# Two blocks of K and V fewer in the third pass: p k vᵀ summed on GpSimd and TensorE in the second

## The chip, the cores and the metric

The kernel runs on one core of a Trainium2 chip. The metric is the device time of one execution in microseconds (us). The core has five engines, each with its own instruction queue: TensorE (PE; its weight loads are shown as PEld), VectorE (DVE), ScalarE (ACT), GpSimd (POOL) and SyncE (SP), and 16 DMA engines between device memory and the on-chip memory SBUF. TensorE writes to PSUM, a small accumulator memory of eight banks.

## What is computed

One decode step (one token, model width 1024) through two rounds of attention and feed-forward, forward and backward:

```python
x = x + A(layernorm(x))      # layer 1: attention, 32 query heads, 4 K/V groups, 65536 keys, head width 128
x = x + B(layernorm(x))      # layer 2: squared-ReLU feed-forward, 1024 -> 3584 -> 1024
x = x + A(layernorm(x))      # layer 3: the same weights and the same caches
x = x + B(layernorm(x))      # layer 4
# outputs: x, and the gradients to the input, k_cache, v_cache, wq, wo, w1, b1, w2, b2

def A(x):
    q = (x @ wq), as 32 heads of 128; k, v = k_cache, v_cache, each group serving 8 heads
    p = softmax(q k^T / sqrt(128)); o = p v
    return o @ wo
```

For a head with the output gradient dO, the gradient to the query is dq = sum over keys c of p_c (dO·v_c − δ) k_c, with δ = dO·o. As dO is the same for all keys, any set of keys S gives

sum over S of p_c (dO·v_c − δ) k_c = (sum over S of p_c k_c v_cᵀ) dO − δ (sum over S of p_c k_c).

The two sums on the right need p, k and v, and neither dO nor δ.

## The kernel before

The caches hold 4 groups x 65536 keys x 128 in bf16, 67 MB each. They do not fit on the chip and are streamed four times:

- **pass 1** (layer 1 forward) and **pass 2** (layer 3 forward), `attn_fwd`: K and V;
- **pass 3** (layer 3 backward, the part that leads to dq of layer 3), `attn_bwd3`: V and K;
- **pass 4** (the rest of layer 1's backward, and the gradients to K and V of both layers), `attn_bwd4`: V and K, and 134 MB are written.

Between the passes lie dense stretches (`dense12`, `dense23`, `dense34`), in which the feed-forward layers run on streamed weights.

**Tiling.** 128 keys are a chunk, 512 chunks are a group. 8 chunks are an item, the step of a pass's loop: a pass has 256 items. 32 chunks (J) are a block of 1 MB, the unit of DMA; two neighbouring blocks that are loaded together are a pair of 2 MB. 64 chunks (HB) make a score tile, 128 chunks (SU) a softmax unit, with a running maximum from unit to unit.

**The arena.** All blocks lie in one SBUF tensor `arena` of 20 granules of 1 MB (`NSLOT` = 12 plus 8). The 8 granules are the planes that keep exp(scores) of each layer and group (`E(lay, g, ...)`), each held from its group's start on until pass 4 has used it. In pass 2 the planes of layer 1 are held throughout and those of layer 3 one after the other, so that K and V have 12 granules and up to three not yet held planes. `kv8` (L351) loads a block or a pair at its first use in program order into the granules that have been free longest (`take_pair`, `take_one`); `kv_done` (L377) gives a block's granule back after its last item, unless the block is in `KV["keep"]`. At the end of pass 2, 7 blocks of V are kept for pass 3. The loads (L361 one block, L366 a pair, L459 weights) are issued from SP's queue in program order; each waits there for its granule's last reader, so that the distance between the release of a granule and its next use is how far a load can run ahead.

**Pass 2.** In `pipeline` (L847) step i runs `kT` of item i (8 transposes of K on PE, L1031, copied from PSUM to a `kt` tile by DVE or ACT, L164 and L161), `kS` of item i−2 (8 score matmuls, L1049), and `v8` of item i−36 (8 matmuls of V with E, L1132), and then `bg.step`: one piece of background work (the q projections of the coming groups, the output projections of the finished ones), if there is any. A unit's statistics (maximum, exponentials) run some steps later: small DVE instructions, two small PE instructions (L1086, L1096) whose PSUM tiles come from `ps_mv` (one buffer, tag `mv`), and the exponentials on ACT (L1114). The order of the instructions on PE, DVE and ACT is the program's order (`manual_schedule`); GpSimd has no work in passes 1 to 3.

**Pass 3.** Step i runs `vT` of item i (8 transposes of V, L1225), `vS` of item i−2 (8 matmuls with dO, L1251), and `k8` of item i−13 (8 matmuls of K with ds = p (dO·v − δ), L1279), which sum dq of one unit in PSUM; `fold` adds the unit to the group's sum with the unit's softmax factor (`fold_dq`).

**Dense23** transposes chunks of the weight w1 into 8 `wt` buffers of its own (`ch_turn`, L1715).

Of the kernel before, what the change touches and what calls it, by code (L numbers as in the profile page):

```python
# [16 lines left out]
P = 128  # L17
# [3 lines left out]
def kernel(  # L21
# [57 lines left out]
    slotp = ctx.enter_context(tc.tile_pool(name="slotp", bufs=1))  # L79


    PS = {}

    def open_psum(stack, name, pass4=False):
        PS["pool"] = stack.enter_context(tc.tile_pool(name=name, bufs=1, space=PSUM))
# [12 lines left out]
        return PS["pool"].tile(shape, F32, name="ps_acc", tag="acc", bufs=1)  # L98

    def ps_mv(shape, dtype=F32):  # L100
        if PS["pass4"]:
            return ps_tr(shape, dtype)
        return PS["pool"].tile(shape, dtype, name="ps_mv", tag="mv", bufs=1)

    def ps_bg(shape):
        return PS["pool"].tile(shape, F32, name="ps_bg", tag="bg", bufs=1)
# [244 lines left out]
    def kv8(t, g, c8):  # L351
        hb, j = divmod(c8, J)
        key = (t, g, hb)
        have = KV["have"]
        if key not in have:
            i = None
            if NOW["pairs"] and hb % 2 == 0 and (t, g, hb + 1) not in have and key not in KV["halves"]:
                i = take_pair()
            if i is None:
                sl = Slot("blk_" + t, load=True)  # L360
                nc.sync.dma_start(out=sl.t.rearrange("p (j d) -> p j d", d=DH), in_=half(KVIN[t], g, hb))  # L361
                have[key] = sl
            else:
                for h in range(2):
                    have[(t, g, hb + h)] = Slot("blk_" + t, at=i + h)
                nc.sync.dma_start(out=wide(i).rearrange("p (j d) -> p j d", d=DH), in_=KVIN[t][g][hb // 2])  # L366
        return have[key].t.rearrange("p (j d) -> p j d", d=DH)[:, j:j + 8, :]
# [9 lines left out]
    def kv_done(t, g, c8):  # L377

        key = (t, g, c8 // J)
        if c8 % J == J - 8 and key not in KV["keep"]:  # L380
            KV["have"].pop(key).free()

    def order_by_unit(desc, unit):
        out = []
        gs = range(G)
        us = range(C // unit)
        for g in (reversed(gs) if desc else gs):
            for u in (reversed(us) if desc else us):
                out += [(g, c8) for c8 in range(u * unit, (u + 1) * unit, 8)]
        return out  # L390
# [18 lines left out]
    DV_LAG = TLEAD + 1  # L409
    V_LEAD = 4 * J // 8  # L410
    ITEMS = [order_by_unit(False, SU), order_by_unit(True, SU), order_by_unit(False, HB), order_by_unit(True, J)]
    V_SHIFT = lambda k: min(V_LEAD, max(0, (k - V_LEAD) // 3))
    TOUCH = [touch_order(ITEMS[0], [("k", 0), ("v", FWD_LAG)]), touch_order(ITEMS[1], [("k", 0), ("v", FWD_LAG)]),
             touch_order(ITEMS[2], [("v", 0), ("k", B3_LAG)]), touch_order(ITEMS[3], [("v", V_SHIFT), ("k", B4_LAG + V_LEAD)])]
# [6 lines left out]
    def start_pass(p):  # L421
        KV["keep"] = plan_keep(p)
        KV["turned"] = KV.get("next", set())
        KV["next"] = set()
        KV["turn"] = {0: "k", 2: "v"}.get(p)
        NOW["pairs"] = p < 3
        KV["halves"] = set(TOUCH[p][-8:] + (TOUCH[p][:18] if p else []))

    def f_cols(ap, nb):
        return ap[:, bass.ds(512 * (nb // 4) + nb % 4, P, step=4)]  # L430
# [353 lines left out]
    class Background:  # L784
# [8 lines left out]
        def step(self, i):  # L793
            while self.later and i >= self.later[0][0]:
                self.add(*self.later.popleft()[1:])
            while self.urgent:
                r = next(self.urgent[0][1], "end")
                if r == "end":
                    self.urgent.popleft()
                    continue  # L800
                if r == "wait":
                    break
                return
            while self.normal and self.done < self.total * i / self.steps:
                if next(self.normal[0], "end") == "end":
                    self.normal.popleft()
                else:
                    self.done += 1
                    return

        def add(self, gen, key=None):
            self.urgent.append((key, gen))
# [27 lines left out]
    def first_at(n, fn):  # L840
        TASKS.setdefault(NOW["i"] + n - 0.5, []).append(fn)
# [2 lines left out]
        for fn in TASKS.pop(i, ()):  # L844
            fn()

    def pipeline(items, stages, bg, end=(), holds=(), lead=None):  # L847

        def due(lag):
            at = {}  # L850
            for k, it in enumerate(items):
                at.setdefault(k + lag + LEAD if lead is None or lag >= 0 else k + ~lag + lead(k), []).append(it)
            return at
        LEAD = 0 if lead is None else lead(len(items))
        when = [due(l) for _, l in stages]
        maxlag = max(l for _, l in stages) + LEAD
        for i in range(len(items) + maxlag):
            NOW["i"] = i
            NOW["wide"] = NOW["pairs"]
            for at, k in holds:  # L860
                if i == at:
                    hold(k)
            tasks(i - 0.5)
            for n, (fn, lag) in enumerate(stages):
                for it in when[n].get(i, ()):
                    fn(*it)
                if n == 0:
                    tasks(i)
            bg.step(max(0, i - LEAD))
            NOW["wide"] = False  # L870
            NOW["step"] += 1
            for before, fn in end:
                if i == len(items) + maxlag - before:
                    fn()
        while TASKS:
            k = min(TASKS)
            NOW["i"] = int(k + 0.5)
            tasks(k)
# [128 lines left out]
    def attn_fwd(p, L, on_group, bg, end=()):  # L1007
# [113 lines left out]
        def v8(g, c8):  # L1121
            su = c8 // SU
            vb8 = kv8("v", g, c8)
            if c8 % SU == 0:
                state["ps_o"] = ps_acc([P, 8, R])
            if c8 % SU == SU // 2:
                unit_sums(g, su)
            ps_o = state["ps_o"]
            for i in range(8):
                c = c8 + i  # L1130
                w = min(8, (su + 1) * SU - c)
                NOW["ps_o"] = nc.tensor.matmul(ps_o[:, 0:w, :], lhsT=vb8[:, i, :], rhs=E(p, g, c, w),  # L1132
                                               start=(c % SU == 0), stop=(c % SU == SU - 1), skip_group_check=True)
            kv_done("v", g, c8)
            if (c8 + 8) % SU == 0:
                first_at(1, lambda: unit_end(g, su, ps_o))

        def unit_sums(g, su):

# [43 lines left out]
        holds = [(k * n + 2, plane(p, g)) for k, g in enumerate(order) if k > 0]  # L1183
        if p == 0:
            holds.append((len(items) - 40, plane(1, ITEMS[1][0][0])))
        with tc.manual_schedule(engines=ORDERED):
            pipeline(items, [(kT, 0), (kS, TLEAD), (v8, FWD_LAG)], bg, end, holds)
        st.close()


# [16 lines left out]
    def attn_bwd3(p, L, on_group, bg, end=()):  # L1207
# [5 lines left out]
        state = {}  # L1213
        gfirst = {g: next(c8 for gg, c8 in items if gg == g) for g in range(G)}
        glast = {g: [c8 for gg, c8 in items if gg == g][-1] for g in range(G)}

        def vT(g, c8):
            bg.need(g)
# [50 lines left out]
        def k8(g, c8):  # L1269
            kb8 = kv8("k", g, c8)  # L1270
            dsT = state[("ds", g, c8 // HB)]
            if c8 % SU == 0:
                state["ps_dq"] = ps_acc([P, 8, R])
            ps_dq = state["ps_dq"]
            for i in range(8):
                c = c8 + i
                s = c % HB
                w = min(8, HB - s)
                nc.tensor.matmul(ps_dq[:, 0:w, :].rearrange("p a b -> p (a b)"), lhsT=kb8[:, i, :],  # L1279
                                 rhs=dsT[:, s:s + w, :].rearrange("p a b -> p (a b)"),  # L1280
                                 start=(c % SU == 0), stop=(c % SU == SU - 1), skip_group_check=True)
            kv_done("k", g, c8)
            if (c8 + 8) % SU == 0:
                su = c8 // SU

                def fold():
                    fold_dq(L, g, su, ps_dq[:, 0, :], gfirst[g] // SU == su, glast[g] // SU == su, dspool)
                    if glast[g] // SU == su:
                        on_group(g)
                first_at(1, fold)  # L1290
# [294 lines left out]

    def open_dense(name):
        st = ExitStack()
        DENSE["pool"] = st.enter_context(tc.tile_pool(name=name, bufs=1))
        return st

# [89 lines left out]
    def on2(g):  # L1680
        if g != lastg[1]:
            bg.add(g_wo(L3, x3, g))
    attn_fwd(1, L3, on2, bg, [(3, pre_load("wo3", lambda: wo_slabs(lastg[1], 2)))])
    bg.drain()

# [29 lines left out]
    def ch_turn(s, js=range(4), to=None):  # L1715

        n = ch_pe(s)
        for j in js:
            pt = ps_tr()
            for kc in range(n):  # L1720
                nc.tensor.transpose(pt[:, kc, :], ch_cols(s, kc, j), ident_b[:, :])
            wt = DENSE["pool"].tile([P, 8, P], BF, name="wt", tag="wt", bufs=8)
            (nc.vector.tensor_copy if (to[j] if to else j == 3) else nc.scalar.copy)(out=wt[:, 0:n, :], in_=pt[:, 0:n, :])
            w1t[(s, j)] = wt

# [132 lines left out]
            bg.add(g_dn(L3, dn3, g, g == firstg[2]))  # L1858
    attn_bwd3(2, L3, on3, bg, [(10, pre_load("wq3", lambda: wq_slabs(lastg[2], 2)))])
    bg.drain()  # L1860


    reset_load()
# [202 lines left out]
```

## Time and profile before

| | |
|---|---|
| median of 3 runs | 1934.61 us (1930.21 to 1937.13) |
| profiled execution: its time; span in the trace | 1938.19 us; 1936.3 us |
| pass 2, first score matmul (L1049) to last V matmul (L1132) | 424.8 to 740.7 us |
| pass 3, first to last matmul with dO (L1251) | 780.0 to 1107.5 us |
| busy share of the span: PE, PEld, DVE, ACT, POOL | 82%, 67%, 61%, 54%, 7% |
| read from device memory, written | 617.62 MB, 165.69 MB |
| mean DMA rate over the span | 407 GB/s |

The page gives one execution: the busy share of each engine, the span in slices, the DMA queues, the chain of work that ended last, and the costliest groups of instructions with what they waited for. A matmul's shown duration is modelled and overlaps with its neighbours'; the spacing of starts tells more than the duration. A window's row gives, for each engine, the busy us and, in brackets, the number of instructions; then the granted clock of TensorE (1.00 is full speed), the DMA share and the rate.

### The profile page before, as it was taken

What the parts mean: (1) busy time and instruction counts of PE and PEld (TensorE: products, weight loads), DVE (VectorE), ACT (ScalarE), POOL (GpSimd) and SP (SyncE); (2) the same over time, 40 slices, a digit from 0 to 9 for tenths busy, and PEclk for the clock granted to TensorE, in tenths of its full rate; (3) what the DMA queues carried; (4) which work ended last, traced back from release to release, by engine and by line L of the source; (5) the groups of instructions that cost most, each with busy time, mean ns of one, the idle gap of its engine ahead of it and who ended that gap; (6) DMA issues with size and microseconds to landing.
All of it is one profiled execution on the core that took longest, in us unless ns stands there. A gap on an engine that the chain in (4) does not pass through costs nothing. (4 is left out here: it accounts for less than half of the span.)

```text
span 1936.3 us, 66770 instructions
## 1 busy us (share of the span) xinstructions
PE 1583.7 (82%) x30099; PEld 1294.0 (67%) x30099; DVE 1172.8 (61%) x2447; ACT 1045.2 (54%) x1620; POOL 143.6 (7%) x325
## 2 busy tenths in 40 slices
PE   6878778588778878978787888778889889688896
PEld 6878777578778878877677776445555556455563
DVE  5645555255555654545454577767867678667685
ACT  3434334245343545436363465757867677567675
POOL 0000000000000000000000002111211111111111
PEclk9989999789998999999999998988988889888896
DMA  9999999999999999999999997999999999999997
GB/s 394 427 427 424 428 429 415 404 421 395 429 425 427 427 419 335 395 426 428 426 420 425 405 363 283 425 422 381 424 424 423 420 399 407 409 415 396 405 421 301
DMA packets 107148, 787.62 MB, mean 407 GB/s; under 512 B 9440, under 2 KB 16622, under 8 KB 42222
## 3 DMA queue, kind: packets, MB, share of 16 engines
q1 hardware_dynamic: 78558, 609.26, 76.2%
q0 software_dynamic: 24080, 165.70, 20.6%
q10 hardware_dynamic: 4224, 8.39, 1.1%
q8 instruction: 235, 3.85, 0.7%
q14 instruction: 51, 0.42, 0.1%
HBM read 617.62 MB, written 165.69 MB: 405 GB/s over the span
## 5 line engine op out<-in xcount | busy, mean ns | idle before, releaser
L164 DVE COPY kt<-ps_tr 128x1024 bf16<-128x1024 bf16 (+1 forms) x733 | 503.3, 688 | 435.7 <-PE ps_tr L1031 237.9
L161 ACT CAST arena<-ps_gg 128x1024 bf16<-128x1024 f32 x457 | 444.4, 1012 | 201.9 <-PE ps_gg L1435 132.0
L1031 PE MATMUL ps_tr<-ident_b,arena 128*128 128x128 bf16 x3840 | 309.1, 225 | 49.3 <-DMA arena<-in_A_k_cache_dram 35.6
L161 ACT COPY kt<-ps_tr 128x1024 bf16<-128x1024 bf16 (+1 forms) x179 | 187.4, 1053 | 185.8 <-PE ps_tr L1225 103.1
L164 DVE CAST arena<-ps_gg 128x1024 bf16<-128x1024 f32 (+2 forms) x186 | 222.3, 1195 | 82.4 <-PE ps_gg L1435 44.4
L1031 PEld LDWEIGHTS <-arena 128*128 128x128 bf16 x3840 | 232.6, 101 | 58.4 <-DMA arena<-in_A_k_cache_dram 38.1
L1132 PE MATMUL ps_acc<-arena 128*128 128x64 bf16 (+4 forms) x4096 | 203.1, 195 | 50.5 <-DMA arena<-in_A_v_cache_dram 32.4
L1435 PE MATMUL ps_gg<-GG,xt 64*128 64x512 bf16 x1024 | 214.3, 414 | 22.0 <-ACT arena L161 10.6
L1354 PE MATMUL ps_tr<-ident_b,arena 128*128 128x128 bf16 x1824 | 179.5, 234 | 38.1 <-DVE kt L164 18.6
L1049 PE MATMUL ps_sc<-L_qpad,kt 128*128 128x64 bf16 (+7 forms) x3584 | 183.1, 194 | 20.8 <-issue 11.0
L1114 ACT ACTIVATE arena<-S_sb,L_negm 128x128 bf16<-128x128 f32 x256 | 165.2, 1006 | 59.4 <-DVE L_negm L1099 51.9
L1132 PEld LDWEIGHTS <-arena 128*128 128x128 bf16 x4096 | 158.2, 100 | 56.6 <-DMA arena<-in_A_v_cache_dram 36.6
L1225 PE MATMUL ps_tr<-ident_b,arena 128*128 128x128 bf16 x2000 | 159.3, 224 | 43.9 <-DMA arena<-in_A_v_cache_dram 42.0
L1354 PEld LDWEIGHTS <-arena 128*128 128x128 bf16 x1824 | 118.9, 104 | 94.2 <-issue 72.8
L1049 PEld LDWEIGHTS <-kt 128*128 128x128 bf16 x3584 | 152.3, 100 | 25.1 <-issue 12.2
L1225 PEld LDWEIGHTS <-arena 128*128 128x128 bf16 x2000 | 120.6, 100 | 49.5 <-DMA arena<-in_A_v_cache_dram 44.7
L1466 PEld LDWEIGHTS <-arena 128*128 128x128 bf16 x2048 | 90.8, 101 | 59.8 <-issue 29.9
L1114 ACT ACTIVATION_READ_ACCUMULATOR arena<-S_sb,L_negm 128x1 f32 x256 | 128.2, 501 | 0.0
L1391 PE MATMUL ps_sc<-DOB,kt 128*128 128x64 bf16 (+3 forms) x1824 | 117.6, 197 | 0.1
L1391 PEld LDWEIGHTS <-kt 128*128 128x128 bf16 x1824 | 84.6, 101 | 48.7 <-issue 47.2
L585 ACT ACTIVATE mv_t<-mv_t 128x1024 bf16<-128x1024 bf16 x96 | 102.0, 1064 | 24.2 <-DVE mv_t L596 24.1
L1466 PE MATMUL ps_acc<-X,arena 128*128 128x64 bf16 (+3 forms) x1536 | 94.7, 197 | 23.5 <-DMA arena<-in_A_k_cache_dram 23.5
(320 smaller groups left out, 2106.0 us busy)
## 6 DMA issues: line engine op xcount, KB each, us to landing
arena<-in_A_k_cache_dram SPq DMA_DIRECT2D x82, 2048.0 KB, 20.7
arena<-in_A_v_cache_dram SPq DMA_DIRECT2D x79, 2048.0 KB, 21.0
out_dram<-arena POOLq DMA_DIRECT2D x149, 1024.0 KB, 15.6
arena<-in_A_v_cache_dram SPq DMA_DIRECT2D x84, 1024.0 KB, 12.5
arena<-in_A_k_cache_dram SPq DMA_DIRECT2D x84, 1024.0 KB, 12.9
arena<-in_A_wo_dram SPq DMA_DIRECT2D x22, 1024.0 KB, 14.9
arena<-in_B_w_dram SPq DMA_DIRECT2D x21, 1024.0 KB, 10.4
arena<-in_A_wq_dram SPq DMA_DIRECT2D x7, 2048.0 KB, 26.2
```

The lines of the kernel that those rows point to most:

```text
L161: nc.scalar.copy(out=out, in_=in_)
L164: nc.vector.tensor_copy(out=out, in_=in_)
L585: nc.scalar.activation(out=t[:, :], in_=t[:, :], func=ACTF.Copy, accum_out=y[:, kc:kc + 1])
L1031: nc.tensor.transpose(pt[:, i, :], kb8[:, i, :], ident_b[:, :])
L1049: nc.tensor.matmul(state["ps_s"][:, s:s + w, :].rearrange("p a b -> p (a b)"), lhsT=kt[:, i, :], rhs=L["qpad"][:, g, 0:w, :].rearrange("p ...
L1114: nc.scalar.activation(out=E(p, g, c0, SU)[:, :, h], in_=S[:, h, :], func=ACTF.Exp, bias=L["negm"][:, g, su, h:h + 1], scale=SCALE, accum_ ...
L1132: NOW["ps_o"] = nc.tensor.matmul(ps_o[:, 0:w, :], lhsT=vb8[:, i, :], rhs=E(p, g, c, w), start=(c % SU == 0), stop=(c % SU == SU - 1), skip ...
L1225: nc.tensor.transpose(pt[:, i, :], vb8[:, i, :], ident_b[:, :])
L1354: nc.tensor.transpose(pt[:, i, :], vb8[:, i, :], ident_b[:, :])
L1391: nc.tensor.matmul(state["ps_dp"][:, s:s + w, :].rearrange("p a b -> p (a b)"), lhsT=vt[:, i, :], rhs=DOB[:, g, 0:w, :].rearrange("p a b - ...
L1435: nc.tensor.matmul(pg[:, 512 * h:512 * h + 512], lhsT=xt[64 * h:64 * h + 64, j1 // 8 + m, :], rhs=gg[64 * h:64 * h + 64, :, :].rearrange(" ...
L1466: nc.tensor.matmul(ps_dq[:, 0:w, :].rearrange("p a b -> p (a b)"), lhsT=kb8[:, i, :], rhs=X[:, s:s + w, :].rearrange("p a b -> p (a b)"), ...
```

## The change

Pass 2 sums, for the unit of 64 chunks that consists of blocks 4 and 5 of its first group (group 3, `MG`, `MU`), m = sum of p k vᵀ for each of the group's 8 heads (`PKV["m"]`, 128 x 8 x 128 in f32) and s = sum of p k (`PKV["s"]`). `g_pkv` is put on a new queue `sides` when `v8` has reached that unit (step 68), and takes one step each time `bg.step` had nothing to issue. For each of the two blocks and each half of the 8 heads it issues 32 GpSimd multiplications p x k (128 x 4 x 128, both operands broadcast, bf16), each followed, two steps later, by a matmul with the 32 chunks' V as weights and 512 columns, summed in PSUM; in the first half also 8 matmuls of 8 columns for p k after every eighth chunk. The sum is copied out by ACT for the first block and added by DVE for the second.

The four blocks (K and V, 4 and 5) are loaded as single blocks, into granules below 12, and are not given back by `kv_done` but by `g_pkv`, at the end of each block. Pass 3 leaves the 8 items of this unit out of its list (248 items); at the first item of the other half of the softmax unit, `pkv_dq` forms m dO − δ s with 8 small f32 matmuls (PE) and two DVE instructions, and `fold` adds it. PSUM's bank of `ps_mv` serves the sum in pass 2 (`ps_m`), and `ps_mv` takes its tiles there from the transposes' three buffers (`ps_tr`). Dense23 takes every other one of its 8 buffers from `ktpool` (4 and 4), which makes room in SBUF for `PKV`.

```diff
     def ps_mv(shape, dtype=F32):
-        if PS["pass4"]:
+        if PS["pass4"] or PS["m"]:
             return ps_tr(shape, dtype)
...
+    def ps_m():
+        return PS["pool"].tile([P, 4, P], F32, name="ps_m", tag="mv", bufs=1)
...
             if i is None:
-                sl = Slot("blk_" + t, load=True)
+                at = None
+                if key in KV["long"]:
+                    at = min((age, i) for i, age in FREE.items() if i < NSLOT)[1]
+                    del FREE[at]
+                sl = Slot("blk_" + t, at=at, load=True)
...
-        if c8 % J == J - 8 and key not in KV["keep"]:
+        if c8 % J == J - 8 and key not in KV["keep"] and key not in KV["long"]:
             KV["have"].pop(key).free()
...
+    MG, MU = ITEMS[1][0][0], 2
+    ITEMS[2] = [(g, c8) for g, c8 in ITEMS[2] if (g, c8 // HB) != (MG, MU)]
+    MKEYS = [(t, MG, hb) for hb in range(MU * HB // J, (MU + 1) * HB // J) for t in "kv"]
...
-            bg.step(max(0, i - LEAD))
+            if not bg.step(max(0, i - LEAD)) and sides:
+                if next(sides[0], "end") == "end":
+                    sides.popleft()
...
+            if p == 1 and (g, c8) == (MG, MU * HB):
+                sides.append(g_pkv(MG, MU))
...
+        def g_pkv(g, u):
+            nc.vector.memset(PKV["s"][:], 0.0)
+            for n, hb in enumerate(range(u * HB // J, (u + 1) * HB // J)):
+                ks, vs = (KV["have"][(t, g, hb)] for t in "kv")
+                k3, v3 = (sl.t.rearrange("p (j d) -> p j d", d=DH) for sl in (ks, vs))
+                for hf in range(2):
+                    acc = ps_m()
+                    made = deque()
+                    def product():
+                        j, r = made.popleft()
+                        nc.tensor.matmul(acc[:, :, :].rearrange("p a b -> p (a b)"), lhsT=v3[:, j, :],
+                                         rhs=r[:, :, :].rearrange("p a b -> p (a b)"), start=j == 0, stop=j == J - 1)
+                    for j in range(J):
+                        r = spool.tile([P, 4, P], BF, name="pk", tag="pk", bufs=3)
+                        e4 = E(p, g, hb * J + j, 1)[:, 0, 4 * hf:4 * hf + 4]
+                        nc.gpsimd.tensor_tensor(out=r[:, :, :], in0=k3[:, j, :].unsqueeze(1).to_broadcast([P, 4, P]),
+                                                in1=e4.unsqueeze(2).to_broadcast([P, 4, P]), op=ALU.mult)
+                        made.append((j, r))
+                        if len(made) > 2:
+                            product()
+                        if hf == 0 and j % 8 == 4:
+                            pk = ps_tr([P, R], F32)
+                            for i in range(8):
+                                jj = j - 4 + i
+                                nc.tensor.matmul(pk[:, :], lhsT=k3[:, jj, :], rhs=E(p, g, hb * J + jj, 1)[:, 0, :], start=i == 0, stop=i == 7)
+                            nc.vector.tensor_tensor(out=PKV["s"][:], in0=PKV["s"][:], in1=pk[:, :], op=ALU.add)
+                        yield
+                    while made:
+                        product()
+                    yield
+                    if n == 0:
+                        nc.scalar.copy(out=PKV["m"][:, 4 * hf:4 * hf + 4, :], in_=acc[:, :, :])
+                    else:
+                        nc.vector.tensor_tensor(out=PKV["m"][:, 4 * hf:4 * hf + 4, :], in0=PKV["m"][:, 4 * hf:4 * hf + 4, :],
+                                                in1=acc[:, :, :], op=ALU.add)
+                for t, sl in (("k", ks), ("v", vs)):
+                    KV["have"].pop((t, g, hb)).free()
+                    KV["long"].discard((t, g, hb))
...
+        def pkv_dq():
+            pt = ps_mv([P, 2, R])
+            for h in range(R):
+                nc.tensor.matmul(pt[:, 0, h:h + 1], lhsT=PKV["m"][:, h, :], rhs=L["dOT"][:, MG * R + h:MG * R + h + 1], start=True, stop=True)
+            nc.tensor.matmul(pt[:, 1, :], lhsT=sel2[:, :], rhs=L["nd2"][:, gsl(MG)], start=True, stop=True)
+            t = dspool.tile([P, R], F32, name="pkv_t", tag="pkv_t", bufs=1)
+            nc.vector.tensor_tensor(out=t[:], in0=pt[:, 1, :], in1=PKV["s"][:], op=ALU.mult)
+            y = dspool.tile([P, R], F32, name="pkv_y", tag="pkv_y", bufs=1)
+            nc.vector.tensor_tensor(out=y[:], in0=pt[:, 0, :], in1=t[:], op=ALU.add)
+            state["pkv"] = y
...
-            wt = DENSE["pool"].tile([P, 8, P], BF, name="wt", tag="wt", bufs=8)
+            DENSE["n"] += 1
+            if DENSE["n"] % 2:
+                wt = ktpool.tile([P, 8, P], BF, name="kt", tag="kt")
+            else:
+                wt = DENSE["pool"].tile([P, 8, P], BF, name="wt", tag="wt", bufs=4)
```

More of the change, by code (lines that the diff above doesn't have):

```diff
@@ L79 @@
     slotp = ctx.enter_context(tc.tile_pool(name="slotp", bufs=1))
-    PS = {}
+    PS = {"m": False}
     def open_psum(stack, name, pass4=False):
@@ L426, in start_pass @@
         NOW["pairs"] = p < 3
-        KV["halves"] = set(TOUCH[p][-8:] + (TOUCH[p][:18] if p else []))
+        KV["halves"] = set(TOUCH[p][-8:] + (TOUCH[p][:18] if p else []) + (MKEYS if p == 1 else []))
+        KV["long"] = set(MKEYS if p == 1 else [])
     def f_cols(ap, nb):
@@ L802, in step @@
                     break
-                return
+                return True
             while self.normal and self.done < self.total * i / self.steps:
@@ L808, in step @@
                     self.done += 1
-                    return
+                    return True
+            return False
         def add(self, gen, key=None):
@@ L845, in tasks, with pipeline @@
             fn()
-    def pipeline(items, stages, bg, end=(), holds=(), lead=None):
+    def pipeline(items, stages, bg, end=(), holds=(), lead=None, sides=()):
         def due(lag):
@@ L1185, in attn_fwd @@
             holds.append((len(items) - 40, plane(1, ITEMS[1][0][0])))
+        sides = deque()
+        PS["m"] = p == 1
         with tc.manual_schedule(engines=ORDERED):
-            pipeline(items, [(kT, 0), (kS, TLEAD), (v8, FWD_LAG)], bg, end, holds)
+            pipeline(items, [(kT, 0), (kS, TLEAD), (v8, FWD_LAG)], bg, end, holds, sides=sides)
+        assert not sides
+        PS["m"] = False
         st.close()
@@ L1215, in attn_bwd3 @@
         glast = {g: [c8 for gg, c8 in items if gg == g][-1] for g in range(G)}
+        sufirst, sulast = {}, {}
+        for g, c8 in items:
+            sufirst.setdefault((g, c8 // SU), c8)
+            sulast[(g, c8 // SU)] = c8
+        def pkv_dq():
[8 more added lines that the diff above has]
+            state["pkv"] = y
         def vT(g, c8):
@@ L1271, in k8 @@
             dsT = state[("ds", g, c8 // HB)]
-            if c8 % SU == 0:
+            su = c8 // SU
+            if c8 == sufirst[(g, su)]:
                 state["ps_dq"] = ps_acc([P, 8, R])
+                if (g, su) == (MG, MU * HB // SU):
+                    pkv_dq()
             ps_dq = state["ps_dq"]
@@ L1280, in k8 @@
                                  rhs=dsT[:, s:s + w, :].rearrange("p a b -> p (a b)"),
-                                 start=(c % SU == 0), stop=(c % SU == SU - 1), skip_group_check=True)
+                                 start=c == sufirst[(g, su)], stop=c == sulast[(g, su)] + 7, skip_group_check=True)
             kv_done("k", g, c8)
-            if (c8 + 8) % SU == 0:
-                su = c8 // SU
+            if c8 == sulast[(g, su)]:
                 def fold():
-                    fold_dq(L, g, su, ps_dq[:, 0, :], gfirst[g] // SU == su, glast[g] // SU == su, dspool)
+                    col = ps_dq[:, 0, :]
+                    if (g, su) == (MG, MU * HB // SU):
+                        both = dspool.tile([P, R], F32, name="pkv_t", tag="pkv_t", bufs=1)
+                        nc.vector.tensor_tensor(out=both[:], in0=col, in1=state["pkv"][:], op=ALU.add)
+                        col = both[:]
+                    fold_dq(L, g, su, col, gfirst[g] // SU == su, glast[g] // SU == su, dspool)
                     if glast[g] // SU == su:
@@ L1587, in open_dense @@
         st = ExitStack()
+        DENSE["n"] = 0
         DENSE["pool"] = st.enter_context(tc.tile_pool(name=name, bufs=1))
@@ L1682, in on2 @@
             bg.add(g_wo(L3, x3, g))
+    PKV = {}
+    pkv_stack = ExitStack()
+    pkv_pool = pkv_stack.enter_context(tc.tile_pool(name="pkv", bufs=1))
+    PKV["m"] = pkv_pool.tile([P, R, P], F32, name="pkv_m")
+    PKV["s"] = pkv_pool.tile([P, R], F32, name="pkv_s")
     attn_fwd(1, L3, on2, bg, [(3, pre_load("wo3", lambda: wo_slabs(lastg[1], 2)))])
@@ L1860 @@
     bg.drain()
+    pkv_stack.close()
     reset_load()
```

## The prediction

> **What bounds the kernel now.** I read the page's slices first, then the DMA issues, then windows of pass 2 and pass 3, the timeline of PE inside pass 2, and the rows of GpSimd.
>
> ```profile
> DMA  9999999999999999999999997999999999999997
> GB/s 394 427 427 424 428 429 415 404 421 395 429 425 427 427 419 335 395 426 428 426 420 425 405 363 283 425 422 381 424 424 423 420 399 407 409 415 396 405 421 301
> ...
> arena<-in_A_k_cache_dram SPq DMA_DIRECT2D x82, 2048.0 KB, 20.7
> arena<-in_A_v_cache_dram SPq DMA_DIRECT2D x79, 2048.0 KB, 21.0
> ```
>
> Each slice is 48.4 us. The DMA engines are taken in nearly every slice, and where nothing disturbs them they move 425 to 429 GB/s. A pair of 2.10 MB takes 2.10 / 0.426 = 4.9 us at that rate but lands 21 us after its issue: some four pairs stand in line. The loads are bound by the rate, with a reserve of about 15 us.
>
> ```profile
> 472.00:702.00 230.00, 185.28 (x4356) 176.61 (x4356) 123.80 (x284) 96.85 (x239) 0.00 (x0) 0.93 1.01 426
> 841.00:1100.00 259.00, 204.06 (x4619) 189.19 (x4616) 127.09 (x244) 118.90 (x162) 0.00 (x0) 0.94 1.01 425
> 790.00:841.00 51.00, 45.82 (x1100) 42.66 (x1097) 29.98 (x59) 26.16 (x35) 0.00 (x0) 1.00 0.99 409
> 700.00:730.00 30.00, 25.03 (x667) 24.01 (x665) 16.12 (x41) 14.74 (x37) 0.00 (x0) 1.00 0.99 414
> ```
>
> Columns after the width: PE, PEld, DVE, ACT, POOL busy, clock, DMA share, GB/s. The first window is the part of pass 2 in which the new work will lie, the second the body of pass 3: both run at the DMA's full rate with PE idle for 45 and 55 us. The last two are stretches in which most granules are kept blocks: 409 and 414 GB/s.
>
> ```profile
> 466.24 0.40 PE L1132 MATMUL ps_acc<-arena 128*128 128x64 bf16 x8
> 466.48 0.61 PE L1031 MATMUL ps_tr<-ident_b,arena 128*128 128x128 bf16 x8
> 466.92 0.35 PE L1049 MATMUL ps_sc<-L_qpad,kt 128*128 128x64 bf16 x8
> 467.13 0.39 PE L1132 MATMUL ps_acc<-arena 128*128 128x64 bf16 x8
> ```
>
> Where data is there, PE does a step in 467.13 − 466.24 = 0.9 us. The pass needs more: the V matmuls (L1132) of 256 items run from 432.4 to 740.7 us, 1.21 us a step. So PE has 0.3 us to spare in a step, and DMA has nothing.
>
> ```profile
> L1363 POOL COPY xin<-arena 128x512 bf16<-128x512 bf16 x64 | 39.8, 622 | 123.9 <-PE ps_tr L1369 102.6 <-PE ps_mv L205 21.0
> L1334 POOL CAST CC<-cf 128x128 bf16<-128x128 f32 x32 | 11.8, 383 | 40.3 <-PE ps_tr L1336 32.6 <-DVE cf L1329 5.1 <-issue 2.5
> ```
>
> These are GpSimd's only arithmetic rows, both of pass 4 and with one operand: 622 ns for 512 elements per partition, 383 for 128.
>
> **The change, part by part.**
>
> *Four block loads less in pass 3.* 4 x 1.049 MB = 4.19 MB, at pass 3's 425 GB/s 9.9 us. PE, DVE and ACT lose 8 of 256 items too, but they are not the bound. Nothing after pass 3 is kept from coming earlier: −9.9 us.
>
> *GpSimd's 128 multiplications.* No row has a multiplication with two operands. Lower end: the copy of the same size, 0.62 us. Upper end: the cast, 383 ns for 128 elements, scaled by 4 elements and 2 operands, 3.1 us. The copy has the same type and size, so I go by it: two reads of 512 elements are 2 x 0.62 = 1.24 us, or 1.04 when the fixed part is paid once (medians 617 and 302 ns give 0.82 ns an element and 197 ns fixed). I take 1.1 us. When does it count? `g_pkv` needs 133 steps and gets those that background work leaves. Two q projections of 10 issuing steps and three output projections of 13 take 59, so it runs from step 68 to about 260, the 230 us of the first window. During the 59 steps GpSimd can run three multiplications ahead in each of five runs, 15 in all; the 59 steps take PE about 1.1 us each, which leaves 230 − 65 = 165 us for 113, so up to 1.46 us each they hide behind the loads. At 1.1 us: 0. PE waits in its own order for a product that is late; behind it stand the transposes, and behind those the release of K's granules.
>
> *PE: 128 products of 512 columns and 64 small matmuls.* The 8 transposes of a step are 1024 columns in 0.44 us (466.48 to 466.92), so 512 columns are 0.22; the shown 0.41 us of other 512-column rows is the far end. 128 x 0.22 = 28 us, and 8 groups of 8 small ones at the 0.24 us of eight V matmuls 2 us. A step with a product is 0.9 + 0.22 = 1.12 us, still below 1.21. Cover: the wait for loads, 45 us in this window against 30. At the far end, 1.31 us a step, 128 x 0.1 = 13 us, partly regained in the other steps. I take 0.
>
> *Granules.* Two K granules are held from step 32 and two V granules from 68; block 4's return at about 165, but each is then half of a pair whose other half is still held, so pair loads have two pairs less until 260. With layer 3's planes held, pairs fall from six to four: two in use, two in line, 10 us of reserve for loads that need 5 us each. Lower end 0. Upper end by the rows with kept blocks, 409 against 426 GB/s: 4% of 230 us, 9 us. These had 5 granules free for a time and four pairs are more: I take 3 us, half of what 414 GB/s would cost.
>
> *Small parts, each at 0.* Two copies of 128x512 f32 on ACT and two adds on DVE (0.75 us, the row of L1055's same shape), in engines idle for 46% and more of the window. `ps_mv` from the transposes' buffers: 24 tiles in a pass, each for about 0.5 us, upper end 2 us if PE has no lead. `pkv_dq`: 8 f32 matmuls at 0.27 (L1096) to 0.46 us with the weight load beside it, 2 to 4 us of PE, covered by the 55 us in pass 3; without cover 4 us. Dense23 keeps 8 buffers in the same order: 0, at most 1 us either way. SP's queue gets four single loads for two pair loads, some 0.35 us each in a queue that waits for granules. No DMA is issued from POOL in pass 2, so the multiplications delay none.
>
> Sum: −9.9 + 3 = −7 us. Span 1936.3 → 1929.4. The profiled execution took 1938.2, 3.6 over the median, so the median 1934.6 goes to **1928 us**.
>
> **Rivals.**
>
> *GpSimd sets the pace (slower).* If a multiplication takes more than 1.46 us, PE waits for every product, and the loads stand behind. At 1.8 us (one and a half times the doubled copy): 113 x 0.34 = 38 us, less 9.9: 1963 us. Each further 0.1 us is 11 us. For it: the cast is dear for its size, and a multiplication has arithmetic that a copy may lack. Against it: the two copies' row.
>
> *DVE kept off by GpSimd.* A unit of 16 steps has five small DVE instructions with two operands from SBUF (L1080, L1102, L1145, L1148, L1150; 157 to 167 ns). If such a one can't run beside a multiplication that reads SBUF, each may wait one multiplication, 1.1 us. The last three follow one another: 3.3 us in which no `kt` copy leaves, while PE's scores need the copy after two steps less its 0.69 us, 1.7 us. PE stands 1.6 us a unit, over 133/16 = 8.3 units 13 us: 1934.6 − 9.9 + 3 + 13 = 1941. In no window of this trace do both engines read so, so nothing here speaks against it, but the two DVE instructions that are alone are covered. The Trainium skill, "SBUF — State Buffer", in its part on the shared port pair, states just this lock: an instruction of VectorE with two SBUF inputs and one of GpSimd that reads SBUF exclude each other for their whole length. No run here shows it yet; by that rule the time would be this rival's.
>
> *Too few granules.* If two pairs in line do not cover the jitter of PE, the upper end of the granules counts, 9 us, and the gain is given back: 1934 us. For it: the 409 GB/s. Against it: with four pairs each load still has 10 us for its 5.
>
> **How the numbers follow.** Forecast 0.44, GpSimd's pace 0.27, DVE kept off 0.15, granules 0.14. A measurement tells 0.3% from no change, 5.8 us. The forecast's own range is 1923 to 1932, of which 0.36 is faster and 0.08 within; granules: 0.01 faster, 0.11 within, 0.02 slower; DVE: 0.05 within, 0.10 slower; GpSimd: 0.01 within, 0.26 slower. Together 0.37, 0.25, 0.38. The range runs from 1922 (nothing given back, 1924.7, and some scatter) to 1966, which leaves out multiplications over 1.83 us.
>
> **What would show it.** Pass 3 should lose 10 us at the same 425 GB/s. In pass 2: starts of the multiplications 1.2 us apart with GpSimd waiting for PE (a late product buffer), not PE waiting for GpSimd; PE idle falling from 45 to some 15 us; the rate at 420 or more. Wrong: PE's products waiting for POOL (GpSimd's pace), the DVE instructions above growing from 0.16 to over 1 us (kept off), or the rate below 412 with pairs landing in 8 us (granules).

## The result, and the profile after

The changed kernel takes **1964.68 us** (median of 4 runs, 1963.29 to 1969.18), against 1934.96 before on the same chips: 1.0161 times, 95% interval 1.0136 to 1.0186. It is slower by 1.6%. The profiled span is 1963.3 us, 27.0 longer. From the first and last starts of the lines that bound each stage:

| stage | before | after | |
|---|---|---|---|
| to the last V matmul of pass 2 | 740.7 | 774.1 | +33.4 |
| dense23, to the first matmul with dO | 39.3 | 40.2 | +0.9 |
| pass 3, to its last matmul of K with ds | 336.6 | 328.0 | −8.6 |
| the rest | 819.7 | 821.0 | +1.3 |

Pass 3 gained what was forecast; pass 2 lost four times as much. The page of the changed kernel, slices and K and V loads:

```profile
POOL 0000000003243462000000002111211112112111
DMA  9999999999988999999999998999999999999997
GB/s 392 427 427 426 426 429 414 407 393 376 390 333 314 407 420 413 341 406 425 429 425 425 411 360 310 425 425 372 424 424 424 418 399 406 410 357 400 425 421 305
...
arena<-in_A_k_cache_dram SPq DMA_DIRECT2D x81, 2048.0 KB, 19.1
arena<-in_A_v_cache_dram SPq DMA_DIRECT2D x77, 2048.0 KB, 17.8
```

The tenth to fourteenth slices (49 us each), with 395 to 429 GB/s before, now move 376, 390, 333, 314 and 407. Windows of the changed kernel, with the columns of the prediction's windows:

```profile
472.00:702.00 230.00, 186.83 (x3955) 168.39 (x3952) 116.22 (x253) 83.53 (x200) 99.64 (x96) 0.91 0.93 369
...
472.00:640.00 168.00, 129.46 (x2681) 117.17 (x2678) 78.53 (x177) 55.49 (x133) 63.35 (x61) 0.89 0.91 354
660.00:760.00 100.00, 91.95 (x2017) 81.16 (x2013) 62.22 (x132) 44.76 (x109) 58.26 (x57) 0.98 1.00 422
```

In the first window PE is idle for 43 us, as much as before, though it has the products to do: it waits for data that the DMA engines, no longer always taken, bring late. But from 660 us on the multiplications run more densely than ever (57 in 100 us) and the loads move 422 GB/s. So the work by itself does not starve them. GpSimd and PE at work:

```profile
L1171 POOL TENSOR_TENSOR pk<-arena 128x512 bf16<-128x512 bf16 x128 | 132.8, 1039 | 216.2 <-PE ps_m L1166 158.5 <-ACT arena L1128 52.4
```
```profile
566.27 0.40 PE L1146 MATMUL ps_acc<-arena 128*128 128x64 bf16 x8
566.50 0.38 PE L1166 MATMUL ps_m<-pk,arena 128*128 128x512 bf16 x1
566.72 0.61 PE L1045 MATMUL ps_tr<-ident_b,arena 128*128 128x128 bf16 x8
567.16 0.40 PE L1063 MATMUL ps_sc<-L_qpad,kt 128*128 128x64 bf16 x8
567.40 0.40 PE L1146 MATMUL ps_acc<-arena 128*128 128x64 bf16 x8
```

A multiplication takes 1.04 us; GpSimd waits 158.5 us for PE to free a product buffer, and PE only 0.4 us in all for GpSimd. A product takes PE 0.22 us (566.50 to 566.72) and a step 1.13. The loads stand in a shorter line. Issues before (480 to 700 us), then after (472 to 702 us):

```profile
arena<-in_A_k_cache_dram SPq DMA_DIRECT2D x20, 2048.0 KB, 20.6
arena<-in_A_v_cache_dram SPq DMA_DIRECT2D x19, 2048.0 KB, 21.1
```
```profile
arena<-in_A_v_cache_dram SPq DMA_DIRECT2D x18, 2048.0 KB, 9.9
arena<-in_A_k_cache_dram SPq DMA_DIRECT2D x17, 2048.0 KB, 10.7
```

A pair lands after 10 us instead of 21: two pairs in line, no longer four. One gap of the changed kernel, SP's issues and then PE:

```profile
602.57 0.33 SPq L373 DMA_DIRECT2D arena<-in_A_k_cache_dram  x1
606.72 0.33 SPq L373 DMA_DIRECT2D arena<-in_A_v_cache_dram  x1
613.93 0.33 SPq L470 DMA_DIRECT2D arena<-in_A_wo_dram  x1
```
```profile
607.41 0.34 PE L527 MATMUL ps_bg<-L_nb,arena 128*128 128x1 bf16 x8
611.83 1.03 PE L1045 MATMUL ps_tr<-ident_b,arena 128*128 128x128 bf16 x8 [4.08 <-DMA arena<-in_A_k_cache_dram]
```

The pair issued at 602.57 is still on its way when PE needs it; PE stands 4.1 us, releases nothing meanwhile, and the next loads are issued late in their turn.

**Why the line is that short** follows from the allocator's rule, worked through pass 2 by hand: the change gives each of its four blocks the granule below 12 that has been free longest, at steps 32, 36, 68 and 72. These are granules 8, 7, 1 and 9. They lie in three different pairs (6–7, 8–9, 0–1), and the fourth shares one of them. So three of the six pairs can't take a pair load; from step 130, when the last plane pair is held, three are left: two in use, one in line. Pair 0–1 becomes whole at step 170, when block 4 is given back, which is where the second half's copy by ACT (L1187) starts, at 645.7 us: just there the rate recovers.

### The profile page after: what moved, and what is told of

Read it like the earlier page. It is cut to its first block, busy times and chain, and to the rows that moved or that the text cites. A ratio compares the mean times of both kernels' runs of the same rounds, so it can differ in the third digit from the quotient of the medians.

```text
span 1963.3 us, 66929 instructions
## 1 busy us (share of the span) xinstructions
PE 1627.7 (83%) x30115; PEld 1315.8 (67%) x30115; DVE 1182.9 (60%) x2455; ACT 1043.8 (53%) x1619; POOL 277.0 (14%) x453
## 5 line engine op out<-in xcount | busy, mean ns | idle before, releaser
L167 DVE COPY kt<-ps_tr 128x1024 bf16<-128x1024 bf16 x728 | 499.1, 688 | 451.9 <-PE ps_tr L1045 258.8
L1045 PEld LDWEIGHTS <-arena 128*128 128x128 bf16 x3840 | 241.7, 101 | 81.9 <-DMA arena<-in_A_k_cache_dram 53.0
L164 ACT COPY kt<-ps_tr 128x1024 bf16<-128x1024 bf16 (+1 forms) x176 | 183.4, 1046 | 205.3 <-PE ps_tr L1302 115.4
L1519 PE MATMUL ps_gg<-GG,xt 64*128 64x512 bf16 x1024 | 218.8, 425 | 18.9 <-ACT arena L164 6.2
L1146 PEld LDWEIGHTS <-arena 128*128 128x128 bf16 x4096 | 158.7, 100 | 47.6 <-DMA arena<-in_A_v_cache_dram 35.5
L1438 PEld LDWEIGHTS <-arena 128*128 128x128 bf16 x1824 | 121.5, 105 | 89.3 <-issue 67.8
L1171 POOL TENSOR_TENSOR pk<-arena 128x512 bf16<-128x512 bf16 x128 | 132.8, 1039 | 216.2 <-PE ps_m L1166 158.5
L1302 PEld LDWEIGHTS <-arena 128*128 128x128 bf16 x1936 | 118.3, 101 | 39.2 <-DMA arena<-in_A_v_cache_dram 35.1
L1550 PEld LDWEIGHTS <-arena 128*128 128x128 bf16 x2048 | 93.4, 103 | 63.1 <-DMA arena<-in_A_k_cache_dram 31.2
L1525 POOL DMA_DIRECT2D out_dram<-arena x128 | 68.3, 534 | 407.8 <-ACT arena L164 246.0
```

What stands on the lines that cost most here:

```text
L164: nc.scalar.copy(out=out, in_=in_)
L167: nc.vector.tensor_copy(out=out, in_=in_)
L1045: nc.tensor.transpose(pt[:, i, :], kb8[:, i, :], ident_b[:, :])
L1171: nc.gpsimd.tensor_tensor(out=r[:, :, :], in0=k3[:, j, :].unsqueeze(1).to_broadcast([P, 4, P]), in1=e4.unsqueeze(2).to_broadcast([P, 4, P] ...
L1302: nc.tensor.transpose(pt[:, i, :], vb8[:, i, :], ident_b[:, :])
L1438: nc.tensor.transpose(pt[:, i, :], vb8[:, i, :], ident_b[:, :])
```

## The experiments

All ratios are to the kernel before on the same chip, with 95% intervals. Theory: the granules, and how they break pairs. Rivals: the work on PE and GpSimd; VectorE kept off by GpSimd.

**Whole pairs.** K of blocks 4 and 5 in one pair, V of them in another.

```diff
+            if key in KV["long"]:
+                both = [(max(FREE[n], FREE[n + 1]), n) for n in range(0, NSLOT, 2) if n in FREE and n + 1 in FREE]
+                i = min(both)[1]
+                del FREE[i], FREE[i + 1]
```

> The change, but the two K blocks share one whole pair of granules and the two V blocks another (one 2 MB load each), so that four pairs stay for pair loads after step 130 where the change leaves three (its four blocks lie in granules 8, 7, 1 and 9, which break three pairs). Broken pairs as the cause: pass 2 runs at 415 GB/s or more again, 1926 to 1934 us. The products on PE or the multiplications on GpSimd as the cause: they are all still there, 1955 to 1966 us. Any hold of four granules costs so much: 1945 to 1960 us.

**Hold only.** `g_pkv` with its steps and its releases, and nothing issued.

```diff
                     for j in range(J):
-                        r = spool.tile([P, 4, P], BF, name="pk", tag="pk", bufs=3)
...
                         yield
```

> The change without any of the work in pass 2: no multiplications, products or small matmuls, the two sums are left at zero; the four granules are held for the same steps, and pass 3 still skips the blocks. Broken pairs as the cause: the loads starve as before, 1948 to 1962 us. Work on PE and GpSimd as the cause: 1925 to 1930 us.

**Work only.** No granule held.

```diff
-        KV["long"] = set(MKEYS if p == 1 else [])
+        KV["long"] = set()
...
-                        nc.tensor.matmul(..., lhsT=v3[:, j, :],
+                        nc.tensor.matmul(..., lhsT=ident_b[:, :],
...
-                        nc.gpsimd.tensor_tensor(out=r[:, :, :], in0=k3[:, j, :].unsqueeze(1)...
+                        nc.gpsimd.tensor_tensor(out=r[:, :, :], in0=ident_b[:, :].unsqueeze(1)...
```

> The change with all of the work in pass 2, but on a constant tile in place of the K and V blocks, so that no granule is held (the sums are those of the constant); pass 3 still skips the blocks. Broken pairs as the cause: 1924 to 1932 us. Work on PE and GpSimd, or DVE kept off by GpSimd, as the cause: 1950 to 1966 us.

**Skip only.** Both edits above together.

> Only the skip: nothing is held and nothing computed in pass 2 (the sums are zero), pass 3 leaves out the four block loads and takes its part from the zero sums. By the loads saved, 4.19 MB at 425 GB/s: 10 us less than before, 1924 to 1927 us. If pass 3 gives part of it back at its ends: 1928 to 1932 us.

| | median us | ratio | interval |
|---|---|---|---|
| the change | 1964.68 | 1.0161 | 1.0136 to 1.0186 |
| whole pairs, with the work | 1941.80 | 1.0023 | 1.0008 to 1.0039 |
| hold only, as the change holds | 1954.18 | 1.0079 | 1.0050 to 1.0108 |
| work only | 1926.85 | 0.9946 | 0.9923 to 0.9969 |
| skip only | 1927.97 | 0.9949 | 0.9927 to 0.9971 |

The work by itself costs nothing (work only is as fast as skip only); the hold costs, with no work at all, and the work on top of the change's hold adds another 0.8%. Keeping the pairs whole takes back 23 us of the 38 that the change has over the work alone. But 1941.80 lies between the two ranges that were expected, so the broken pairs are the larger part of the loss and not all of it. The window 472 to 702 us of work only, then of hold only (the traced run, 1946.88 us, is the shortest of its four), then of whole pairs:

```profile
472.00:702.00 230.00, 203.32 (x4526) 182.79 (x4524) 137.22 (x292) 98.63 (x241) 118.42 (x114) 0.97 1.01 425
```
```profile
472.00:702.00 230.00, 172.83 (x3945) 166.71 (x3942) 111.38 (x255) 88.61 (x217) 0.00 (x0) 0.90 0.95 382
```
```profile
472.00:702.00 230.00, 195.08 (x4285) 175.08 (x4283) 129.41 (x279) 92.77 (x222) 113.05 (x109) 0.96 0.97 396
```

425 GB/s with all of the work, 382 with none of it. Whole pairs still lose 14 us against skip only, where the prediction gave two pairs 3 us. So the next four ask for the price of a pair.

**Block pairs.** K and V of one block in the halves of one pair.

```diff
+                    if hb not in KV["at"]:
+                        both = [(max(FREE[n], FREE[n + 1]), n) for n in range(0, NSLOT, 2) if n in FREE and n + 1 in FREE]
+                        KV["at"][hb] = min(both)[1]
+                        del FREE[KV["at"][hb]], FREE[KV["at"][hb] + 1]
+                    at = KV["at"][hb] + (t == "v")
```

> The change, but K and V of block 4 lie in the two halves of one pair, K and V of block 5 in those of another, so that the end of block 4 (step 170) gives a whole pair back: pairs left for pair loads are five to step 130, four to step 170, five to 259, where the whole pairs of K and of V left four from 130 to 259. If the pairs left set the pace: 1930 to 1937 us, between the version with whole pairs of K and of V (1942) and the one that holds nothing (1927). If the number of held granules counts and not how they lie: two of four come back at step 170 in the change as well, and nothing changes against whole pairs of K and of V, 1940 to 1945 us.

**The same, a step of g_pkv in each step.**

```diff
-            if not bg.step(max(0, i - LEAD)) and sides:
+            bg.step(max(0, i - LEAD))
+            if sides:
```

> As the version with block pairs, and g_pkv takes a step in each step of the pass, beside the background work too, so that block 4 is given back at step 134 and block 5 at 200: five pairs to step 200, six after. If the pairs left set the pace: 1926 to 1932 us, faster than before. If PE can't carry a product and a piece of background work in one step (0.9 + 0.2 + 0.3 us against 1.2): 1933 to 1942 us.

**Whole pairs, hold only.** The first experiment with the second's `g_pkv`.

> Whole pairs of K and of V held as in the first experiment, with no multiplications, products or small matmuls (the sums are zero). If the hold alone costs: 1936 to 1943 us, near the 1942 with work. If it is the work on PE in a short reserve, which delays each release: 1927 to 1933 us.

**One pair gone.** Skip only, and a whole pair taken out of the free list at step 32, given back by the last step of `g_pkv`.

> Only the skip, with no work in pass 2 (the sums are zero), and one whole pair of granules taken out of use from step 32 to 259: five pairs left after step 130. If pairs left set the pace and five are enough: 1926 to 1930 us, as with nothing held. If every pair counts: 1932 to 1938 us.

| | median us | ratio | interval |
|---|---|---|---|
| block pairs | 1943.76 | 1.0041 | 1.0022 to 1.0059 |
| block pairs, each step | 1930.85 | 0.9986 | 0.9971 to 1.0002 |
| whole pairs, hold only | 1938.48 | 1.0026 | 1.0010 to 1.0041 |
| one pair gone, no work | 1926.58 | 0.9964 | 0.9948 to 0.9980 |

Without work, then, 0, 1, 2 and 3 pairs gone give 0.9949, 0.9964, 1.0026 and 1.0079: little for the first pair, some 15 us for two, some 25 us for three, where two and three are the same four granules, placed otherwise. Block pairs missed what was expected of the theory: a pair that comes back at step 170 did not help, and 1943.76 lies in the range of the other case, that only the number of held granules counts. That number can't be the whole cause, as the change holds just as many for the same steps and takes 23 us longer than whole pairs. The trace shows where block pairs lose: 321 and 348 GB/s in 600 to 620 and 620 to 640 us, with the return at 629.4, and 426 from 640 to 660. So most of it is lost before the pair comes back. Shortening the hold did help (1930.85), though not beyond doubt against the kernel before.

**Single loads.** If broken pairs cost, loads that need no pair should not feel them. One line, in three kernels: block pairs with a step in each step, the change itself, and the kernel before. (Weights are then loaded into single granules in pass 2 too.)

```diff
-        NOW["pairs"] = p < 3
+        NOW["pairs"] = p in (0, 2)
```

> The version with block pairs and a step of g_pkv in each step, and pass 2 loads every block alone (1 MB) in place of pairs: a granule is free again as soon as its block is done, not when both of a pair are, so that about two granules more stand in line. If the reserve of granules is what is left to lose: 1924 to 1930 us. If 1 MB loads cost rate: 1932 to 1940 us.

> The change itself, with single block loads in all of pass 2: its four held granules can't break a pair any more. If the broken pairs made the loss: 1926 to 1940 us. If the work of the change in a short reserve made it, whatever the loads: 1950 to 1966 us.

> The kernel before with single block loads in all of pass 2, for the price of single loads alone: 1931 to 1938 us if it is nothing (the granules do not limit it), more if 1 MB loads move fewer bytes a microsecond.

| | median us | ratio | interval |
|---|---|---|---|
| block pairs, each step, single loads | 1933.15 | 0.9999 | 0.9983 to 1.0014 |
| the change, single loads | 1926.42 | 0.9964 | 0.9949 to 0.9979 |
| before, single loads | 1937.43 | 1.0017 | 1.0002 to 1.0032 |

With this line the change is **faster than the kernel before by 0.36%**, and 11 us faster than that kernel with the same line. It holds the same number of blocks for the same steps, and does the same work. Single loads change two things at once: they need no whole pair, and a granule is free as soon as its own block is done. This run does not part the two; the version with whole pairs, which loads pairs as the change does, shows what the breaking alone costs. The window of the change with single loads, and its landings there:

```profile
472.00:702.00 230.00, 204.84 (x4593) 183.89 (x4590) 135.04 (x295) 101.23 (x243) 118.80 (x115) 0.99 1.01 423
```
```profile
arena<-in_A_v_cache_dram SPq DMA_DIRECT2D x42, 1024.0 KB, 18.4
arena<-in_A_k_cache_dram SPq DMA_DIRECT2D x41, 1024.0 KB, 17.8
```

A load of half the size lands 18 us after its issue: some seven blocks in line, where the change with pairs had two pairs, four blocks. Block pairs with a step of `g_pkv` in each step, which helped with pair loads, is 7 us slower than that and outside the 1924 to 1930 us that were expected of it; why was not tried.

## Why the prediction was wrong

- **Four block loads less in pass 3, −9.9 us: right.** Pass 3 is 8.6 us shorter; the skip alone is worth 0.51% (0.29 to 0.73), 10 us.
- **GpSimd, 1.1 us a multiplication, hidden: right.** 1.04 us, and GpSimd waits for PE. The rival that gives it the pace is out, although its price, 1963 us, lies next to the result: the right number from the wrong cause.
- **PE, 0.22 us a product, hidden: right as long as the line is long.** 0.22 us, and work only shows no cost. In a short line it is not quite free: the change is 0.8% over hold only. With two whole pairs held the total shows no such difference (1.0023 with work, 1.0026 without), though between 660 and 690 us the loads move 389 GB/s with the work, PE busy for 28.2 of the 30 us, and 428 without.
- **"Pairs fall from six to four ... I take 3 us": the step that failed, twice.** I took "each is then half of a pair" to mean two pairs, without following which granule each block gets. The rule picks the oldest granule, with no regard to its neighbour, and breaks three pairs. And the price for two pairs was too small as well: some 15 us measured (10 to 20 by the intervals), over the upper end of 9. I took that end from stretches with kept blocks. Of the loads issued there, 6 of 15 (790 to 841 us) and 11 of 13 (700 to 730) are single ones, which need no pair, so these rows could not price pairs. Nor did I count the weights, which take granules too. Worked through by the same rule, in the version with whole pairs those of steps 144 and 176 (issued at 567.9 and 614.5 us) take a whole pair and later half of one, so that three pairs are left and not four: 376 GB/s between 580 and 660 us. Those of steps 231 and 240 (689.0 and 703.8 us) lie in the odd halves that block 4 gave back, and break none: 426 between 700 and 740. No run tries the weights by themselves.
- **The rival "too few granules"** was the right mechanism, with too low a price (1934 us).
- **VectorE kept off:** the stall is there, the loss is not. In pass 2 the four lines L1094, L1116, L1202 and L1207 take 16.8 us instead of some 7.9, single ones of 8 elements up to 0.99 us for 0.17:

```profile
L1207 DVE TENSOR_TENSOR z<-zn,rs 128x8 f32<-128x8 f32 x12 | 6.5, 539 | 1.3 <-ACT arena L1128 0.9
...
563.79 2.04 POOL L1171 TENSOR_TENSOR pk<-arena 128x512 bf16<-128x512 bf16 x2 [13.77 <-PE ps_m L1166]
565.02 0.83 DVE L1202 TENSOR_TENSOR o_t<-oacc,al 128x8 f32<-128x8 f32 x1
```

  The DVE instruction at 565.02 us ends at 565.85, just when the second of the two multiplications does (565.83). The Trainium skill's lock ("SBUF — State Buffer", "Who interferes with whom") is borne out by these rows. But work only has the stall too and loses nothing: 9 us spread over pass 2 stay behind DVE's idle time.
- **Small parts at 0: right.** Dense23 and the rest add 2 us; the matmuls of `pkv_dq` take 1.7 us (1103.2 to 1104.9), under the 2 to 4 expected.

What would have shown it was named: pairs landing in 8 us and a rate below 412. They came as 10 us and 369.

## What to carry to other kernels

When a change holds on to a buffer of a pool that feeds a saturated DMA, follow the allocator to the buffers it really takes, and count what is left in whole units of a load, not in bytes. A reserve is not an average: price it in the stretch where the fewest buffers are left, and count everything that takes them, here the weights too. If held buffers fragment the pool, smaller loads can be worth more than their own cost: here 0.17% for single loads against 2% regained.

## What the hardware showed that was not expected

A wait is paid twice. After PE's 4.1 us at 611.83 its eight transposes show 1.03 us in place of 0.61, and the next instructions start 0.82 us after them in place of 0.45. The mean granted clock of the starved window 472 to 640 is 0.89 against 0.98 from 660 on (0.93 before the change, 472 to 640): late data leaves a slower engine. That it then releases its granules later still is an inference. The Trainium skill ("TensorE: Matmul & The Clock Gate", Part 1) states that the clock falls when the array has been idle for about 3.4 us; this wait is longer, and the row behind it agrees. What share of the 33 us the slower clock has, no run separates.
